# Reordering the first two rows' sums, one transfer's issuer and the first norm in a one-core state-space and MLP kernel

## The chip, the core and the metric

The kernel runs on one core of one Trainium2 chip. The metric is the device time of one execution in microseconds, as the median of several executions; less is better. A profiled execution gives, beside its own time, the span from the first to the last instruction and the record of every instruction.

## What is computed

There are two blocks on a sequence of 2048 positions with 448 channels, cut here to what matters:

```python
x = A_q
h = x + A_ref(layernorm(x), k, v, shift_k, ssm_k, ssm_D)   # q * (long convolution of k_shift*v)
h2 = h + B_ref(layernorm(h), w1, b1, w2, b2)
# B_ref: layernorm, then over the positions: gelu(h^T w1 + b1), 1792 wide, then times w2, plus b2
```

The first block is a causal convolution over all 2048 positions (the reference does it by FFT) of `k_shift * v` with a long filter, plus `kv * ssm_D`, multiplied by the normalised `q`. The second block normalises again, twice in the reference, and runs a two-layer MLP along the positions.

## The kernel before, in words

The 2048 positions lie as 128 partitions by 16 "rows" (R = 16; row r holds the positions 16q + r), each row 448 channels wide. The convolution is done as transforms written as matmuls: stage 1 and stage 2 for the filter and for the input, products, and a first inverse stage ("i1", `emit_products_i1`), which goes over eight pairs of blocks. Each pair's result is copied from PSUM to the SBUF tile TU by ScalarE (line 738) and from there rearranged by SBUF-to-SBUF transfers into the tile TZ (line 1200; for the last pair line 1189). The transfers of one pair but the last carry both halves of the data (h = 0 and 1) in one go; the last pair's go out one for each half and each block of the pair, four in all. Before, GpSimd issues one of these four (h = 1, first block) and SP three (h = 1 second block, then the two of h = 0).

The second inverse stage ("i2", `emit_i2`) makes, for each row r, one sum in PSUM: two matmuls over TZ (line 1299, h = 0 and 1). Rows 0 and 1 (NZ = 2) are special: their share of the last pair isn't moved into TZ, it is added by four more matmuls (line 1307) that read TU in place, with weights EW. "In-place matmuls" means these. Then come, row by row:

- rows 0 to 3: VectorE combines the sum, straight from PSUM, with a normalised x that was prepared ahead (line 1337). What is prepared (XN) is made by ScalarE (line 1269) from statistics (VectorE, lines 1236 and 1238), a power on GpSimd (lines 1244 and 1247), a product on GpSimd (line 1256) and one on VectorE (line 1259).
- rows 4 to 15: ScalarE (for some rows VectorE) first gates the sum from PSUM (line 1316 or 1318), then VectorE combines (line 1326).
- the second norm of the row: for rows 0 and 1 each, VectorE takes statistics (line 1343), aggregates (line 1346) and forms the variance (line 1375), GpSimd takes the power (line 1379), and VectorE writes the normalised row Q (line 1385). The other rows go in pairs: the combine also accumulates a sum, which is read by a short second instruction (DVE_READ_ACCUMULATOR), ScalarE squares with an accumulator (line 1355), GpSimd does the small arithmetic (lines 1365 to 1379), and VectorE writes Q.

From row 8 on, a row's sum may not start before the gate of the row before it has ended (`after=av[-1:]`, line 1301). The MLP's first layer starts while these rows are still made: with each row's Q, TensorE adds that row's share to seven sums in PSUM (line 1432), seven matmuls a row; then the other seven sums (line 1442) and the second layer (line 1453), whose results VectorE adds to x (line 1456) and which go out.

The order of each engine's work is written out by hand in the table `ORDER`: for each engine a list of tokens such as `i2.1:0-1`, that is stage tag, step number and the numbers of the operations in that step. The program issues them on the engine in just this order; waits follow from the data. A small planner runs over these lists with estimated costs only to choose PSUM banks and the order of emission. The tokens that the change touches: in "pe", `ct.1:7` is a transpose of a table, `warm.2` a matmul whose result isn't used, `i2.1` and `i2.2` belong to row 0, `i2.9` and `i2.10` to row 1, `i2.28`, `i2.45`, `i2.17` to rows 4, 7 and 2. In "dve", `q.N` are the statistics of x (`q.7` rows 12 and 13, `q.8` rows 14 and 15; even numbers are the statistics op, odd ones the aggregate), `i2.3` to `i2.8` belong to row 0 (combine 3, statistics 4, aggregate 5, variance 6, norm 8), `i2.11` to `i2.16` to row 1 in the same way, `i2.18` and `i2.21` are the combines of rows 2 and 3, `i2.26` and `i2.27` their norms, `i2.30` and `i2.34` the combines of rows 4 and 5. In "pool" and "sp", `i1.16:19` to `i1.16:22` are the last pair's four transfers, `q.2:5` is the power for rows 2 and 3, `xn.3:0` the product behind it.

Of the kernel before, what the change touches and what calls it, by code (L numbers as in the profile page):

```python
# [39 lines left out]
    ),  # L40
    "act": (
# [24 lines left out]
    ),  # L66
    "pool": (
# [10 lines left out]
    ),  # L78
# [8 lines left out]
    ),  # L87
}

# [493 lines left out]
def _build(nc, A_q, A_k, A_v, A_shift_k, A_ssm_k, A_ssm_D, B_w1, B_b1, B_w2, B_b2, out):  # L583
# [5 lines left out]
    Bsz, S, D = A_q.shape  # L589
# [5 lines left out]
    DB = 2 * D  # L595
# [23 lines left out]
    o_TU = 104064  # L619
# [18 lines left out]
    with ctx:  # L638
        sch = _Sched(nc, ctx, n_dma_sems=112, small_off=SMALL)
        op = sch.op  # L640
# [25 lines left out]
        TU = view(o_TU, [R, 2, D])  # L666
        KN = view(o_KN, [4, S])
        W2 = [view(o, [NFC // 2, S]) for o in o_W2]
        TZ = view(o_TZ, [R, 2, D])
# [3 lines left out]
        ET = view(o_ET, [2 * R, 128], f16)  # L673
# [11 lines left out]
        NZ = 2  # L685
        o_EW = o_I2 + 128
        EW = view(o_EW, [4 * NZ, 128], f16)
# [24 lines left out]
        def Pb(b, i=0):  # L712
            return PS[:, b.slots[i], 0:D]
# [164 lines left out]
        r_ET = lambda r: (o_ET + 512 * r, 512)  # L878
# [271 lines left out]
        def emit_products_i1():  # L1150
            for jj in range(R // 2):
                ms = []
                for h in range(2):
# [10 lines left out]
                       r=[ru, (o_TK + i * 2 * DB, 2 * DB)], bw=[m], n=4 * D, after=aft)  # L1164
# [8 lines left out]
                for h in range(2):  # L1173
                    for t, (tab, xy) in enumerate(((mt[0], 0), (mt[2], 3), (mt[1], 1), (mt[1], 2))):
                        for par in range(2):
                            P = slice(64 * par, 64 * par + 64)
                            k = op("pe", lambda e, W, b=bs[h], m=ms[h], par=par, t=t, tab=tab, xy=xy, P=P: e.matmul(  # L1177
                                Pb(b, par), tab[P, :], MR(m.slots[0])[P, xy, :], start=(t == 0), stop=(t == 3)),
                               r=r_iv if jj < R // 2 - 1 else [(o_ML, 768)], br=[ms[h]], bw=[bs[h]], n=D, est=94.5, mode=3)
# [3 lines left out]
                if jj == R // 2 - 1:  # L1183
                    for h in range(2):
                        for par in range(2):
                            j = 2 * jj + par
                            p0 = 64 * (j & 1) + 32 * ((j >> 1) & 1) + (j >> 2)
                            o_h = o_TU + (2 * j + h) * DB
                            k = op("pool" if h and par == 0 else "sp", lambda e, W, j=j, h=h, p0=p0: e.dma_start(
                                TZ[p0:p0 + 29:4, NZ:R, h, :], TU[0:8 * (R - NZ), j, h, :]),  # L1190
                                   r=[(o_h, DB)], w=[(o_TZ + NZ * 2 * DB, (14 - NZ) * 2 * DB, "zpool"), (o_TZ + 28 * DB, 4 * DB, "zsp")],
                                   dmab=8 * (R - NZ) * DB, keng=8)
                            shuf["zpool"] = k
                            shuf.setdefault("zl", []).append(k)
                    continue
                for par in range(2):
                    j = 2 * jj + par
                    p0 = 64 * (j & 1) + 32 * ((j >> 1) & 1) + (j >> 2)
                    for q_, a, b_, j0 in (("sp" if j in (1, 3, 5, 9, 11) else "pool", 0, 112, 0), ("pool" if jj in (2, 3, 6) else "sp", 112, 128, 14)):
# [3 lines left out]
                           r=[(o_TU + j * 2 * DB, 2 * DB)], w=[(o_TZ + j0 * 2 * DB, (b_ - a) // 8 * 2 * DB, "zsp" if j0 else "zpool")],  # L1203
# [79 lines left out]
        def emit_i2():  # L1283
            sch.t0 = T_M1 + 30.0
            op("pool", lambda e, W: e.tensor_tensor(out=bm, in0=qs[:, :, 0], in1=b2c, op=ALU.add),
               r=[(o_qst, 256), (o_b2c, 64)], w=[(o_bm, 64)], n=16)
            av = []
            first = []
            for g, (r0, ng) in enumerate(GR):
                oh = o_hst + 64 * g  # L1290
                hs = view(oh, [16], f32)
                for i in range(ng):
                    r = r0 + i
                    sch.t0 = T_I2 + T_DI2 * r
                    b = _Buf(psum)
                    A = view(o_TZ + r * 2 * DB, [D], f32)
                    tz = [(o_TZ + r * 2 * DB, 2 * DB)]
                    for h in range(2):
                        k = op("pe", lambda e, W, b=b, r=r, h=h: e.matmul(  # L1299
                            Pb(b), ET[:, 2 * r + h, :], TZ[:, r, h, :], start=(h == 0), stop=(h == 1 and r >= NZ)),  # L1300
                           r=[r_ET(r)] + tz, bw=[b], n=D, after=av[-1:] if r >= 8 and h == 0 else ())
                    if r < NZ:
                        sch.t0 += 0.2
                        for h in range(2):
                            for jx in range(2):
                                j = R - 2 + jx
                                k = op("pe", lambda e, W, b=b, r=r, h=h, j=j, jx=jx: e.matmul(  # L1307
                                    Pb(b), EW[:, 4 * r + 2 * jx + h, :], TU[:, j, h, :], start=False, stop=(h == 1 and jx == 1)),
                                   r=[(o_EW + 1024 * r + 512 * jx + 256 * h, 256), (o_TU + (2 * j + h) * DB, DB)], bw=[b], n=D, safter=(k,))
                    i2_last.append(k)  # L1310

                    sch.t0 += 0.01
# [27 lines left out]
                    if ng == 1:  # L1340
# [3 lines left out]
                           r=hx, w=[(oh + 32, 24)], n=D, kind="1x")  # L1344
# [6 lines left out]
                    else:  # L1351
# [6 lines left out]
                           r=hx, w=[(oh + 8 + 4 * i, 4), (o_JK, DB)], n=D, est=580.0)  # L1358
# [3 lines left out]
                if ng == 2:  # L1362
# [4 lines left out]
                       r=[(oh, 8)], w=[(oh + 16, 8)], est=290.0)  # L1367
                    op("pool", lambda e, W, hs=hs: e.tensor_tensor(out=hs[:, 6:8], in0=hs[:, 4:6], in1=hs[:, 4:6],
                                                                   op=ALU.mult), r=[(oh + 16, 8)], w=[(oh + 24, 8)], est=290.0)
                    op("pool", lambda e, W, hs=hs: e.tensor_tensor(out=hs[:, 8:10], in0=hs[:, 2:4], in1=hs[:, 6:8],  # L1370
                                                                   op=ALU.subtract),
# [10 lines left out]
                for i in range(ng):  # L1382
                    r = r0 + i
# [132 lines left out]
```

## Time and profile before

| | us |
|---|---|
| median of 3 runs | 172.06 |
| lowest and highest of them | 171.93, 172.31 |
| the profiled execution's own time | 172.93 |
| its span, first to last instruction | 171.0 |

Over the span TensorE's matmuls are busy 162.0 us (95%), its weight loads 95.1, VectorE 98.9, ScalarE 92.9 and GpSimd 60.3. The granted TensorE clock is 1.0 throughout. A row of the timeline gives start and duration in us, the engine, the line of the kernel, the operation, what is written and read, and how many like instructions follow one another; a bracket behind it gives idle time of the engine ahead of it and what ended that. PE is TensorE's matmul, PEld its weight load, DVE VectorE, ACT ScalarE, POOL GpSimd, SPq SyncE's queue. Instructions overlap a little in their engine's pipeline, so the step from one start to the next can be shorter than a duration.

### The profile page before, as it was taken

The numbers are of one execution on the slowest core, as the hardware profiler recorded it, in microseconds if no ns is written. First come the engines' busy times: TensorE is split into PE (matmuls) and PEld (weight loads), VectorE is DVE, ScalarE is ACT, GpSimd is POOL, SyncE is SP. The second block draws the span as 40 slices with busy tenths as digits, with TensorE's granted clock in tenths as the row PEclk, the third lists the DMA queues.
The fourth block names the chain that finished last, engine by engine and source line by source line (L and its number), as shares of the span: only waits on it lengthen the run. The fifth ranks groups of instructions, "written<-read, shape, count | busy, mean of one in ns | idle before, by whom it ended". The sixth has DMA issues, their size and how long they took to land.

```text
span 171.0 us, 3568 instructions
## 1 busy us (share of the span) xinstructions
PE 162.0 (95%) x1425; PEld 95.1 (56%) x1425; DVE 98.9 (58%) x187; ACT 92.9 (54%) x133; POOL 60.3 (35%) x154
## 2 busy tenths in 40 slices
PE   6989999988889999999999999999999999999993
PEld 2766745442334443464455555555567777777783
DVE  7988988869699999999968810000003223132232
ACT  3698787998889999999887437321210000000000
POOL 8346627591810496576888820000000000000000
PEclk9999999999999999999999999999999999999999
DMA  5999677675859667665999999970000111101111
GB/s 167 406 310 384 192 246 274 246 281 210 270 147 372 236 182 217 186 185 183 319 361 404 413 419 421 418 324 13 0 0 4 54 54 54 54 0 58 54 54 54
DMA packets 15740, 35.15 MB, mean 206 GB/s; under 512 B 3628, under 2 KB 9980, under 8 KB 15724
## 3 DMA queue, kind: packets, MB, share of 16 engines
q1 hardware_dynamic: 12924, 29.08, 47.2%
q0 software_dynamic: 2656, 5.76, 10.5%
q8 instruction: 11, 0.18, 0.4%
q10 hardware_dynamic: 144, 0.08, 0.2%
q14 instruction: 5, 0.04, 0.1%
HBM read 22.05 MB, written 1.84 MB: 140 GB/s over the span
## 4 chain that ended last, share of the span: by engine, by line
PE 66%; ACT 14%; DMA 12%; DVE 3%; issue 2%; SPq 2%; POOL 0%; DVEq 0%
PE ps L1453 25%; PE ps L1442 12%; PE ps L1432 11%; ACT arena L738 7%; DMA arena<-arena 7%; DMA arena<-in_A_ssm_k_dram 5%; PE ps L1094 5%; ACT arena L1069 4%; PE ps L1177 4%; PE ps L1059 2%; PE ps L1299 2%; ACT arena L1316 2%; PE ps L992 1%; DVE arena L742 1%; PE ps L1307 1%
## 5 line engine op out<-in xcount | busy, mean ns | idle before, releaser
L1456 DVE SCALAR_TENSOR_TENSOR arena<-ps,arena 128x448 bf16<-128x448 f32 (+2 forms) x17 | 11.2, 656 | 57.4 <-PE ps L1453 57.3
L1453 PE MATMUL ps<-arena 128*128 128x448 bf16 (+2 forms) x238 | 42.7, 342 | 0.0
L1453 PEld LDWEIGHTS ps<-arena 128*128 128x128 bf16 x238 | 33.3, 145 | 9.5
L738 ACT CAST arena<-ps 128x896 bf16<-128x896 f32 x30 | 24.6, 1021 | 0.5 <-PE ps L1094 0.5
L1432 PE MATMUL ps<-arena 128*128 128x448 bf16 x112 | 22.5, 353 | 0.0
L1069 ACT CAST arena<-ps 128x896 bf16<-128x896 f32 x24 | 20.5, 915 | 3.7 <-PE ps L1059 3.7
L1075 POOL DMA_DIRECT2D arena<-arena x32 | 17.6, 553 | 12.7 <-ACT arena L1069 11.1
L1442 PE MATMUL ps<-arena 128*128 128x448 bf16 x112 | 21.3, 352 | 0.0
L1422 ACT ACTIVATE arena<-ps,arena 128x448 bf16<-128x448 f32 x14 | 8.2, 639 | 18.7 <-PE ps L1442 14.6
L1094 PE MATMUL ps<-arena 128*64 128x448 bf16 x128 | 15.2, 359 | 2.9 <-ACT arena L1069 0.9
L1160 DVE TENSOR_TENSOR arena<-arena 128x1792 bf16<-128x1792 bf16 x16 | 16.7, 1086 | 0.3 <-ACT arena L738 0.3
L1432 PEld LDWEIGHTS ps<-arena 128*128 128x128 bf16 x112 | 10.8, 98 | 10.6 <-DVE arena L1385 0.9
L1442 PEld LDWEIGHTS ps<-arena 128*128 128x128 bf16 x112 | 11.0, 98 | 10.2
L1059 PE MATMUL ps<-arena 128*32 128x448 bf16 x256 | 15.0, 355 | 0.8 <-DVE arena L1007 0.5
L1177 PE MATMUL ps<-arena 64*128 64x448 bf16 x128 | 14.5, 351 | 0.1
L1200 POOL DMA_DIRECT2D arena<-arena x15 | 8.7, 583 | 13.8 <-ACT arena L738 13.8
L1094 PEld LDWEIGHTS ps<-arena 128*64 128x64 f16 x128 | 6.2, 108 | 10.8 <-ACT arena L738 3.0
L1177 PEld LDWEIGHTS ps<-arena 64*128 64x128 f16 x128 | 6.1, 94 | 8.2 <-ACT arena L738 2.5
L1007 DVE TENSOR_TENSOR arena<-ps,arena 128x512 bf16<-128x512 f32 (+1 forms) x16 | 9.1, 618 | 2.1 <-PE ps L992 1.8
L1355 ACT ACTIVATE arena<-arena 128x448 bf16<-128x448 bf16 x14 | 8.0, 572 | 3.7 <-DVE arena L1326 3.6
L738 ACT COPY arena<-ps 128x1024 bf16<-128x1024 bf16 (+1 forms) x8 | 8.1, 1073 | 3.3 <-PE ps L966 3.3
L1059 PEld LDWEIGHTS ps<-arena 128*32 128x32 f16 x256 | 5.1, 95 | 7.6 <-DVE arena L1007 2.5
(97 smaller groups left out, 194.4 us busy)
## 6 DMA issues: line engine op xcount, KB each, us to landing
arena<-in_B_w_dram SPq DMA_DIRECT2D x8, 896.0 KB, 9.5
arena<-in_B_w_dram SPq DMA_DIRECT2D x2, 2048.0 KB, 17.8
arena<-arena POOLq DMA_DIRECT2D x32, 112.0 KB, 3.1
arena<-arena SPq DMA_DIRECT2D x16, 224.0 KB, 3.3
arena<-in_B_w_dram SPq DMA_DIRECT2D x2, 1536.0 KB, 20.3
arena<-in_A_k_dram SPq DMA_DIRECT2D x4, 448.0 KB, 6.0
arena<-in_A_v_dram SPq DMA_DIRECT2D x4, 448.0 KB, 9.0
arena<-in_A_q_dram SPq DMA_DIRECT2D x4, 448.0 KB, 5.5
```

The lines of the kernel that those rows point to most:

```text
L738: return e.copy(out=dst(), in_=src())
L1007: return e.tensor_tensor(out=v, in0=u.rearrange("p t (r d) -> p t r d", d=64), in1=v, op=ALU.mult)
L1059: op("pe", lambda e, W, b=b, r=r, q=q, x=x, c0=c0: e.matmul(PS[32 * q:32 * q + 32, b.slots[x], 0:D], E[:, 2 * r + x, c0:c0 + 32], src[:, r ...
L1069: return e.copy(out=dst, in_=Ppair(b)) if W == "act" else e.tensor_copy(out=dst, in_=Ppair(b))
L1075: shuf[tag].append(op(q_, lambda e, W, g=g, i=i, a=a, nu=nu, jh=jh: e.dma_start(T[a + i:a + i + 4 * nu - 3:4].rearrange("p (j k) c d -> p ...
L1094: op("pe", lambda e, W, b=bs[h], h=h, j=j, c=c, par=par: e.matmul(PS[64 * par:64 * par + 64, b.slots[c], 0:D], FW[:, 64 * c:64 * c + 64], ...
L1160: op("dve", lambda e, W, m=m, i=i: e.tensor_tensor(out=MR(m.slots[0]).rearrange("p (x y) d -> p x y d", x=2), in0=TU[:, i].unsqueeze(2).br ...
L1177: k = op("pe", lambda e, W, b=bs[h], m=ms[h], par=par, t=t, tab=tab, xy=xy, P=P: e.matmul(Pb(b, par), tab[P, :], MR(m.slots[0])[P, xy, :], ...
L1432: op("pe", lambda e, W, r=r, fc=fc, b=bs[fc]: e.matmul(Pb(b), W1A[:, r, 128 * fc:128 * fc + 128], Q[:, r, :], start=(r == 0), stop=(r == R ...
L1442: op("pe", lambda e, W, r=r, fc=fc, b=b: e.matmul(Pb(b), W1B[:, r, 128 * (fc - n0):128 * (fc - n0) + 128], Q[:, r, :], start=(r == 0), sto ...
L1453: op("pe", lambda e, W, r=r, fc=fc, b=b, d0=d0, d1=d1: e.matmul(Pb(b)[:, d0:d1], W2[fc // 7][:, fc % 7, r:S:R], G[:, fc, d0:d1], start=(fc ...
L1456: op("dve", lambda e, W, r=r, b=b, d0=d0, d1=d1: e.scalar_tensor_tensor(out=X[:, r, d0:d1], in0=Pb(b)[:, d0:d1], scalar=bm[:, r:r + 1], in ...
```

## The change

It has three parts. First, for rows 0 and 1 the four in-place matmuls are issued ahead of the two over TZ, with h = 1 ahead of h = 0, and the first of them opens the sum; TensorE's list has row 0's six, then row 1's six in this order, and the transpose `ct.1:7` goes ahead of them. Second, of the last pair's four transfers GpSimd issues the two of the first block (h = 1, then h = 0), the latter placed ahead of `q.2:5`; SP issues the other two. Third, in VectorE's list the statistics op of row 13 (`q.7:2`) leaves its place ahead of row 0's combine and goes behind the combine of row 5 (`i2.34`); row 0's statistics, aggregate and variance come ahead of row 1's combine; row 0's norm comes ahead of the combine of row 2; and `q.8:2` goes behind the norm of row 2 (`i2.26`).

The diff, cut in the long lists to the tokens that move:

```diff
 "pe":
-ct.2:0-7 warm.12:0 warm.3:0 ct.0:0-7 ct.1:0-6 warm.2:0 i2.1:0-1 i2.2:0-3 i2.9:0 ct.1:7 i2.9:1 i2.10:0-3
+ct.2:0-7 warm.12:0 warm.3:0 ct.0:0-7 ct.1:0-7 warm.2:0 i2.1:0-3 i2.2:0-1 i2.9:0-3 i2.10:0-1
 "dve":
-xn.3:1 q.7:0 q.7:2 i2.3:0 q.6:3 i2.4:0 i2.11:0 i2.5:0
-i2.12:0 i2.6:0 i2.13:0 i2.18:0 i2.14:0 i2.8:0 i2.21:0 i2.16:0 i2.30:0 i2.34:0 q.7:1 q.7:3 q.8:0 q.8:2
-i2.26:0 q.8:1 q.8:3 i2.27:0
+xn.3:1 q.7:0 i2.3:0 q.6:3 i2.4:0 i2.5:0 i2.6:0 i2.11:0
+i2.12:0 i2.13:0 i2.8:0 i2.14:0 i2.18:0 i2.21:0 i2.16:0 i2.30:0 i2.34:0 q.7:2 q.7:1 q.7:3 q.8:0 i2.26:0 q.8:2
+q.8:1 q.8:3 i2.27:0
 "pool":
-q.2:4 i1.16:21 q.2:5
+q.2:4 i1.16:21 i1.16:19 q.2:5
 "sp":
-i1.16:22 i1.16:20 i1.16:19 w1a.1:0
+i1.16:22 i1.16:20 w1a.1:0
@@ emit_products_i1
-k = op("pool" if h and par == 0 else "sp", lambda e, W, j=j, h=h, p0=p0: e.dma_start(
+k = op("pool" if par == 0 else "sp", lambda e, W, j=j, h=h, p0=p0: e.dma_start(
     TZ[p0:p0 + 29:4, NZ:R, h, :], TU[0:8 * (R - NZ), j, h, :]),
@@ emit_i2
-for h in range(2):
-    k = op("pe", lambda e, W, b=b, r=r, h=h: e.matmul(
-        Pb(b), ET[:, 2 * r + h, :], TZ[:, r, h, :], start=(h == 0), stop=(h == 1 and r >= NZ)),
-       r=[r_ET(r)] + tz, bw=[b], n=D, after=av[-1:] if r >= 8 and h == 0 else ())
 if r < NZ:
-    sch.t0 += 0.2
-    for h in range(2):
+    k = None
+    for h in (1, 0):
         for jx in range(2):
             j = R - 2 + jx
             k = op("pe", lambda e, W, b=b, r=r, h=h, j=j, jx=jx: e.matmul(
-                Pb(b), EW[:, 4 * r + 2 * jx + h, :], TU[:, j, h, :], start=False, stop=(h == 1 and jx == 1)),
+                Pb(b), EW[:, 4 * r + 2 * jx + h, :], TU[:, j, h, :], start=(h == 1 and jx == 0), stop=False),
...
+    sch.t0 += 0.2
+for h in range(2):
+    k = op("pe", lambda e, W, b=b, r=r, h=h: e.matmul(
+        Pb(b), ET[:, 2 * r + h, :], TZ[:, r, h, :], start=(h == 0 and r >= NZ), stop=(h == 1)),
+       r=[r_ET(r)] + tz, bw=[b], n=D, after=av[-1:] if r >= 8 and h == 0 else ())
```

More of the change, by code (lines that the diff above doesn't have):

```diff
@@ L1307, in emit_i2 @@
                                 k = op("pe", lambda e, W, b=b, r=r, h=h, j=j, jx=jx: e.matmul(
-                                    Pb(b), EW[:, 4 * r + 2 * jx + h, :], TU[:, j, h, :], start=False, stop=(h == 1 and jx == 1)),
-                                   r=[(o_EW + 1024 * r + 512 * jx + 256 * h, 256), (o_TU + (2 * j + h) * DB, DB)], bw=[b], n=D, safter=(k,))
+                                    Pb(b), EW[:, 4 * r + 2 * jx + h, :], TU[:, j, h, :], start=(h == 1 and jx == 0), stop=False),
+                                   r=[(o_EW + 1024 * r + 512 * jx + 256 * h, 256), (o_TU + (2 * j + h) * DB, DB)], bw=[b], n=D,
+                                   safter=() if k is None else (k,))
+                        sch.t0 += 0.2
[3 more added lines that the diff above has]
+                           r=[r_ET(r)] + tz, bw=[b], n=D, after=av[-1:] if r >= 8 and h == 0 else ())
                     i2_last.append(k)
```

52 rows, old and new, of the table ORDER are left out of this document.

## The prediction, on record before the result was known

> **What bounds the kernel now.** I read the page first (TensorE is busy nearly throughout), then the windows, to find where TensorE stops waiting for anything, then the chain that ended last and the timeline just ahead of that point. The windows count each engine's busy time in a stretch; TensorE is the second column.
>
> ```profile
> core 0 of [0], span 171.0 us
> ...
> 84.12:125.75 41.63, 41.63 (x222) 21.55 (x222) 11.82 (x37) 18.19 (x39) 12.95 (x32) 1.00 0.75 295
> 125.75:168.40 42.65, 42.65 (x239) 33.13 (x237) 10.64 (x16) 0.63 (x1) 0.00 (x0) 1.00 0.11 41
> ```
>
> From 84.12 us on TensorE is full to its last matmul, at a granted clock of 1.00. The work behind that point is the same before and after, so the change is worth just what it moves that point. The timeline ahead of it (start, duration, engine, line, idle time in brackets):
>
> ```profile
> 79.33 0.55 POOL L1379 TENSOR_TENSOR arena<-arena 128x1 f32<-128x1 f32 x1 [0.50 <-DVE arena L1375]
> 79.34 0.65 DVE L1337 SCALAR_TENSOR_TENSOR arena<-ps,arena 128x448 bf16<-128x448 f32 x1
> 79.91 0.08 DVE L1337 DVE_READ_ACCUMULATOR arena<-ps,arena 128x1 f32 x1
> ...
> 79.98 0.39 DVE L1385 TENSOR_SCALAR arena<-arena 128x448 bf16<-128x448 bf16 x1
> 80.03 0.58 ACT L1355 ACTIVATE arena<-arena 128x448 bf16<-128x448 bf16 x1
> ...
> 80.28 0.68 DVE L1337 SCALAR_TENSOR_TENSOR arena<-ps,arena 128x448 bf16<-128x448 f32 x1
> 80.42 0.87 PEld L1432 LDWEIGHTS ps<-arena 128*128 128x128 bf16 x6 [0.45 <-DVE arena L1385]
> ...
> 82.94 0.71 ACT L1316 ACTIVATE arena<-ps,arena 128x448 f32<-128x448 f32 x1
> ...
> 83.70 0.11 PEld L1299 LDWEIGHTS ps<-arena 128*128 128x128 f16 x2 [0.52 <-ACT arena L1316]
> ...
> 83.71 0.55 PE L1299 MATMUL ps<-arena 128*128 128x448 bf16 x2
> ...
> 84.12 1.06 PEld L1432 LDWEIGHTS ps<-arena 128*128 128x128 bf16 x7 [0.30 <-DVE arena L1385]
> ```
>
> Read it backwards. Row 10's sum (83.71) waits for ScalarE's gate of row 9, which ends at 82.94 + 0.71 = 83.65. ScalarE runs without a gap from row 2's square (80.03) to that gate. The square squares what VectorE's combine of row 2 (79.34) writes; the read of that combine's accumulator ends at 79.91 + 0.08 = 79.99, and the square starts 0.04 later. So the chain is: combine of row 2, square, ScalarE's queue, row 10's sum, end. The 0.45 us at 80.42, where TensorE waits for the first norm, lies ahead of the stop at 83.70 and costs nothing of its own.
>
> **The change, part by part.** First the start of the stage: transfers, TensorE and GpSimd.
>
> ```profile
> 72.12 1.87 ACT L738 CAST arena<-ps 128x896 bf16<-128x896 f32 x2
> ...
> 73.20 2.19 SPq L1189 DMA_DIRECT2D arena<-arena  x3
> ...
> 73.47 0.63 POOL L1189 DMA_DIRECT2D arena<-arena  x1 [0.63 <-ACT arena L738]
> ...
> 74.13 0.74 POOL L1247 TENSOR_TENSOR arena<-arena 128x2 f32<-128x2 f32 x1
> ...
> 74.56 0.35 PE L1210 MATMUL ps<-arena 128*128 128x448 f16 x1
> 74.95 0.19 POOL L1256 TENSOR_TENSOR arena<-arena 128x2 f32<-128x2 f32 x1
> ...
> 75.28 0.54 PE L1299 MATMUL ps<-arena 128*128 128x448 bf16 x2 [0.36 <-DMA arena<-arena]
> ...
> 75.42 1.07 POOL L1247 TENSOR_TENSOR arena<-arena 128x4 f32<-128x4 f32 x1
> ...
> 75.65 0.92 PE L1307 MATMUL ps<-arena 128*128 128x448 bf16 x4
> ...
> 77.50 0.95 PEld L1299 LDWEIGHTS ps<-arena 128*128 128x128 f16 x6 [0.18 <-DMA arena<-arena]
> ```
>
> ```profile
> DMA to landing us min/median/max: 2.8/2.8/2.8
> ```
>
> *Matmul order.* Four in-place matmuls start 0.19 us apart (0.92 for four, the last 0.35 long: 0.57 over three starts). They read only what ScalarE's casts leave, so they no longer wait for the landing that holds row 0 until 75.28. The trace has no such start; it is bounded by the last warm-up matmul: 0.25 after its start if a transpose and one slot lie between (74.81), or after its end if the sum gets its PSUM bank (74.56 + 0.35 + some 0.1 = 75.03). I take 75.03, since the old sum too started only behind it. Row 0's last matmul then ends at 75.03 + 5 x 0.19 + 0.35 = 76.33 (early end 76.11), instead of 75.65 + 0.92 = 76.57.
>
> *GpSimd's second transfer.* The casts end at 72.12 + 1.87 = 73.99. SP's three issues take 2.19 (about 0.7 each), so its third starts near 74.72 and lands 2.8 later, at 77.5, which is what TensorE's load of row 4 waits for at 77.50. GpSimd started its issue 0.27 after SP for the same cast. So its second starts at 74.29, takes 0.63, and lands at 77.1: rows 2 and up are 0.4 sooner. But everything queued behind it on GpSimd is later. The power of rows 2 and 3 (L1247) moves from 74.13 to 74.95, the product (L1256) from 74.95 to 75.77; both have readers on VectorE and ScalarE.
>
> ```profile
> 73.70 2.12 ACT L738 COPY arena<-ps 128x1024 f16<-128x1024 f16 x2
> ...
> 75.46 0.13 DVE L1259 SCALAR_TENSOR_TENSOR arena<-arena 128x2 f32<-128x2 f32 x1
> ...
> 75.50 1.14 DVE L1236 BATCH_NORM_STATS2 arena<-arena 128x6 f32<-128x448 bf16 x2
> 75.62 1.46 ACT L1269 ACTIVATE arena<-arena 128x448 f32<-128x448 bf16 x2
> ...
> 76.61 0.68 DVE L1337 SCALAR_TENSOR_TENSOR arena<-ps,arena 128x448 bf16<-128x448 f32 x1
> ...
> 76.94 1.05 ACT L738 COPY arena<-ps 128x1024 f16<-128x1024 f16 x1
> 77.21 0.17 DVE L1238 BATCH_NORM_AGGREGATE arena<-arena 128x2 f32<-128x6 f32 x1
> 77.33 0.63 DVE L1343 BATCH_NORM_STATS2 arena<-arena 128x6 f32<-128x448 bf16 x1
> 77.47 0.24 POOL L1244 TENSOR_SCALAR arena<-arena 128x4 f32<-128x4 f32 x1 [0.97 <-DVE arena L1238]
> ...
> 77.79 1.04 POOL L1247 TENSOR_TENSOR arena<-arena 128x4 f32<-128x4 f32 x1
> 77.87 0.67 DVE L1337 SCALAR_TENSOR_TENSOR arena<-ps,arena 128x448 bf16<-128x448 f32 x1
> ...
> 78.18 0.72 ACT L1316 ACTIVATE arena<-ps,arena 128x448 f32<-128x448 f32 x1 [0.19 <-PE ps L1299]
> ```
>
> *What that wait holds.* L1259 needs the power, which now ends at 75.69: it starts at 75.73 instead of 75.46. Behind it in VectorE's queue stands one statistics op (0.54 start to start) before row 0's combine, where two stood: the combine can start at 75.77 + 0.54 = 76.31. TensorE allows 76.33 + 0.04. I take 76.35, 0.26 sooner than 76.61. ScalarE's two activations (L1269) need the product, so they move from 75.62 to 76.00 and the copy behind them to 77.31; a copy takes about 0.9 start to start (2.12 for two), so the gate of row 4 starts at 78.22 instead of 78.18, although its sum is there sooner. The transfer's gain ends here.
>
> *VectorE's order* is the large term. From row 0's combine to row 2's it now does everything of row 0 first, in a chain where each op needs the one before. An op that needs its predecessor starts 0.04 after that one's end (76.61 + 0.68 = 77.29, then 77.33); one that doesn't starts 0.09 ahead of it (77.33 + 0.63 = 77.96, but 77.87). The sum: combine 0.68 + 0.04; statistics 0.63 + 0.04; aggregate 0.17 + 0.04; variance 0.07 (79.91 to 79.98 holds one such op); combine of row 1 0.67 + 0.04; statistics 0.63 + 0.04; aggregate 0.10; norm of row 0 0.30 (79.98 to 80.28); variance of row 1 0.07: 3.52 us, where before it was 79.34 - 76.61 = 2.73. So row 2's combine starts at 76.35 + 3.52 = 79.87 instead of 79.34: **0.53 us later**.
>
> The norm inside that sum must not wait for its power. GpSimd's group that ends at 75.42 + 1.07 = 76.49 is 0.82 later, 77.31; the next group, 77.79 + 1.04 - 77.47 = 1.36 long if it starts at once, ends near 78.7; the power of row 0 (L1379, 0.55) at about 79.3. VectorE comes to the norm at 79.5. That cover is some 0.15 us; any more delay on GpSimd passes straight to the end.
>
> *The small moves.* The transpose that goes ahead of row 0 is counted above (one slot at 74.75). The statistics op taken from in front of combine 0 comes back behind the combine of row 5, where another one leaves for a place behind the norm of row 2: that norm has as many ops ahead of it as before, and the norm of row 3 one more (0.54), which TensorE needs only after the seven matmuls of the 84.12 row, 1.3 us later. GpSimd's group for rows 4 to 7 ends at 77.31, ahead of the gate of row 4. SP drops an issue and starts its next weight load up to 0.4 sooner; nothing in the stretch waits for it. If one of these covers fell, its price would be its own delay, at most 0.5.
>
> *Sum.* Square of row 2 at 80.56; ScalarE's unbroken queue keeps its length of 83.65 - 80.03; row 10's sum at 84.24. TensorE's work ahead of it starts sooner, but only waits longer there. The second stop, 84.12 for the norm of row 2, hangs on the square of row 3 in the same queue and moves by at most as much. So +0.53: the profiled execution of 172.93 us (span 171.0 and 1.93 around it) would be 173.46. The median of the runs shown, 172.06, lies 0.87 below that execution, so the forecast is 172.06 + 0.53 = 172.59. Its own range, with combine 0 between 76.1 and 76.6, is 172.3 to 172.8.
>
> **One rule weighed.** The rows above price the dependence of one VectorE op on the last at 0.13 us. The Trainium skill, "VectorE: DVE Perf Modes", section "The DRAIN you can't avoid", says that the next op waits for an empty pipe in any case and that a semaphore after each op costs nothing extra. By that rule the chain costs only its ops; the 77.87 row, which starts ahead of its predecessor's end, speaks against it here.
>
> **The rivals.**
>
> *B, the order costs only its ops.* If dependent ops follow like the others, the sum is 2.73 plus the norm (0.30) and a variance (0.07) that now come first: 3.10, combine 2 at 79.45, +0.1: 172.2. The starts above speak against it, the short distance for it.
>
> *C, faster: ScalarE's queue starts sooner.* If combine 2 doesn't end last, the queue starts with row 4's sum. That is ready when its transfer lands: 77.1 against 77.5, so up to 0.4 sooner, 171.65. It decides from the point where combine 2 starts ahead of 79.34 and L1269 isn't late; combine 0 would have to start by 75.84, and row 0's matmuls end only after 76.1. Against it also is that GpSimd's issue delays L1269.
>
> *D, GpSimd's second issue is held or lands late.*
>
> ```profile
> 81.19 0.68 DVE L1326 SCALAR_TENSOR_TENSOR arena<-arena 128x448 bf16<-128x448 bf16 x1
> ...
> 81.45 0.47 POOL L1368 TENSOR_TENSOR arena<-arena 128x2 f32<-128x2 f32 x1
> ...
> 84.02 0.19 POOL L1368 TENSOR_TENSOR arena<-arena 128x2 f32<-128x2 f32 x1
> ```
>
> The same small GpSimd op takes 0.19 alone and 0.47 beside VectorE's combine, ending 0.05 after it. If a statistics op of 0.61 held the issue so, the power, combine 0 and all behind would be up to 0.6 later again: 173.1. The first issue, 0.63 at 73.47 beside such an op, shows no hold. The Trainium skill, "SBUF — State Buffer", section "Who interferes with whom", has GpSimd blocked only by VectorE ops with two SBUF inputs or in a two-port mode, which would clear the statistics ops. A late landing alone is covered: row 4's sum may be 0.4 later before ScalarE, which waits for combine 2, notices.
>
> That the transfer moves without effect (nothing is gained at 77.5) is part of the forecast already.
>
> **Chances.** Forecast 0.62, B 0.16, C 0.11, D 0.11. A measurement of this kernel tells about 0.2%, 0.34 us, from no change. Faster by more: C, 0.11. Within: B and the forecast's low edge, 0.21. Slower: the rest and D, 0.68. The range takes in B, the forecast and the nearer part of D, and the spread of the runs: 171.95 to 172.95.
>
> **What would show it.** Right: combine 2 (the third L1337) near 79.87; ScalarE idle before its first square (L1355), released by VectorE; row 10's sum (L1299) near 84.2; L1259 and L1269 later by 0.3 to 0.4. Wrong: combine 2 at or before 79.4, or a first square that starts right behind the gates. If TensorE showed a new stop behind 84.2, or none at row 10, the whole chain would be misread.

## The result, and the profile after

The changed kernel takes 173.00 us (median of 22 runs, 172.18 to 175.25) where the kernel before takes 172.38 us in the same comparison (22 runs, 171.61 to 173.66). The ratio is 1.0031 with a 95% interval of 1.0016 to 1.0046, that is 0.53 us slower (0.28 to 0.79). The ratio leaves out the run of 175.25 us, whose granted clock was 0.99, so it differs a little from that of the two medians. The prediction was 0.53 us slower. The kernel before measured 0.32 us higher here than in the three runs that were shown, so the absolute 173.00 lies 0.41 above the predicted 172.59 and 0.05 above the upper end of the range, 172.95; with the same 0.32 added, the range is 172.27 to 173.27, and 173.00 lies in it. The difference is what was predicted. The profiled execution of the changed kernel took 173.51 us, span 171.5.

In the changed kernel the lines behind 1290 lie up to two further down: 1303 are the in-place matmuls, 1309 the two over TZ, 1318 the gate, 1328 and 1339 the combines, 1345, 1348, 1377 and 1381 the statistics, aggregate, variance and power of rows 0 and 1, 1357 the square, 1387 the norm, 1434 the MLP's first layer. First the windows of the kernel after, behind the last place where TensorE stops for long:

```profile
84.50:126.18 41.68, 41.68 (x221) 21.48 (x220) 12.09 (x38) 18.12 (x40) 12.12 (x31) 1.00 0.74 291
126.18:168.80 42.62, 42.62 (x239) 33.12 (x237) 10.61 (x16) 0.63 (x1) 0.00 (x0) 1.00 0.11 41
```

TensorE is full from there on as before, with the same work to do (before, two stretches of 41.63 and 42.65 us). So the loss arose ahead of 84.50. The timeline of the kernel after, from the last transfers on:

```profile
72.08 1.87 ACT L738 CAST arena<-ps 128x896 bf16<-128x896 f32 x2
...
74.25 0.60 POOL L1189 DMA_DIRECT2D arena<-arena  x1 [0.19 <-issue]
...
74.77 0.92 PE L1303 MATMUL ps<-arena 128*128 128x448 bf16 x4
74.86 0.74 POOL L1247 TENSOR_TENSOR arena<-arena 128x2 f32<-128x2 f32 x1
...
75.52 0.54 PE L1309 MATMUL ps<-arena 128*128 128x448 bf16 x2
75.63 0.16 DVE L1259 SCALAR_TENSOR_TENSOR arena<-arena 128x2 f32<-128x2 f32 x1
...
75.91 1.41 ACT L1269 ACTIVATE arena<-arena 128x448 f32<-128x448 bf16 x2
...
76.25 0.67 DVE L1339 SCALAR_TENSOR_TENSOR arena<-ps,arena 128x448 bf16<-128x448 f32 x1
...
76.95 0.63 DVE L1345 BATCH_NORM_STATS2 arena<-arena 128x6 f32<-128x448 bf16 x1
...
77.61 0.18 DVE L1348 BATCH_NORM_AGGREGATE arena<-arena 128x2 f32<-128x6 f32 x1
...
77.66 1.10 PE L1309 MATMUL ps<-arena 128*128 128x448 bf16 x5 [0.46 <-DMA arena<-arena]
77.83 0.15 DVE L1377 TENSOR_SCALAR arena<-arena 128x1 f32<-128x1 f32 x1
77.90 0.68 DVE L1339 SCALAR_TENSOR_TENSOR arena<-ps,arena 128x448 bf16<-128x448 f32 x1
```

The time from issue to landing of the two transfers that GpSimd issues:

```profile
DMA to landing us min/median/max: 2.9/3.0/3.1
```

And from where TensorE has row 4's sum to the point from which it is full:

```profile
78.61 0.63 DVE L1345 BATCH_NORM_STATS2 arena<-arena 128x6 f32<-128x448 bf16 x1
...
79.28 0.18 DVE L1348 BATCH_NORM_AGGREGATE arena<-arena 128x2 f32<-128x6 f32 x1
79.38 0.36 DVE L1387 TENSOR_SCALAR arena<-arena 128x448 bf16<-128x448 bf16 x1
79.66 0.15 DVE L1377 TENSOR_SCALAR arena<-arena 128x1 f32<-128x1 f32 x1
79.72 0.67 DVE L1339 SCALAR_TENSOR_TENSOR arena<-ps,arena 128x448 bf16<-128x448 f32 x1
...
80.30 1.30 PE L1434 MATMUL ps<-arena 128*128 128x448 bf16 x6
...
80.44 0.58 ACT L1357 ACTIVATE arena<-arena 128x448 bf16<-128x448 bf16 x1 [0.25 <-DVE arena L1339]
...
81.77 0.55 PE L1309 MATMUL ps<-arena 128*128 128x448 bf16 x2 [0.17 <-ACT arena L1318]
...
83.35 0.71 ACT L1318 ACTIVATE arena<-ps,arena 128x448 f32<-128x448 f32 x1
...
84.11 0.11 PEld L1309 LDWEIGHTS ps<-arena 128*128 128x128 f16 x2 [0.68 <-ACT arena L1318]
```

Read it forwards. What the new orders on TensorE and VectorE were to bring sooner is sooner: row 0's combine starts at 76.25 (before 76.61), its norm at 79.38 (before 79.98), and TensorE takes up the first layer at 80.30 without a stop (before 80.42, behind a stop of 0.45). But the combine of row 2 starts at 79.72 instead of 79.34. ScalarE, which before came to its first square just as the combine ended, now idles for it (0.25 us, released by L1339), and from the square on its queue runs without a gap to the gate of row 9. TensorE's weight load for row 10's sum waits for that gate, 0.68 us instead of 0.52, and the sum starts at 84.12. Row 9's sum (81.77) now has a stop of its own, 0.17 us behind the gate of row 8 in the same queue. It adds nothing, because TensorE stops again for the gate of row 9.

The two executions differ a little ahead of this stage, so distances are taken from the end of ScalarE's last cast of the products: 72.12 + 1.87 = 73.99 before and 72.08 + 1.87 = 73.95 after. Row 10's sum starts 9.72 us behind it before and 10.17 after: **0.45 us later**, which is the loss. The same distance tells the experiments apart below, more finely than their times do: one comparison's interval is 0.4 us to either side.

### The profile page after: what moved, and what is told of

The parts are those of the page before. It is cut to its first block, busy times and chain, and to the rows that moved or that the text cites. A ratio compares the mean times of both kernels' runs of the same rounds, so it can differ in the third digit from the quotient of the medians.

```text
span 171.5 us, 3568 instructions
## 1 busy us (share of the span) xinstructions
PE 162.3 (95%) x1425; PEld 95.1 (55%) x1425; DVE 99.2 (58%) x187; ACT 93.0 (54%) x133; POOL 59.7 (35%) x155
## 4 chain that ended last, share of the span: by engine, by line
PE 64%; ACT 13%; DMA 9%; DVE 6%; POOL 2%; issue 2%; SPq 2%; DVEq 0%; POOLq 0%
PE ps L1455 25%; PE ps L1444 12%; PE ps L1434 11%; ACT arena L738 7%; DMA arena<-in_A_ssm_k_dram 5%; PE ps L1094 5%; DMA arena<-arena 5%; ACT arena L1069 4%; PE ps L1177 4%; PE ps L1059 2%; PE ps L992 1%; PE ps L1309 1%; DVE arena L742 1%; ACT arena L1357 1%; DVE arena L1339 1%
## 5 line engine op out<-in xcount | busy, mean ns | idle before, releaser
L1236 DVE BATCH_NORM_STATS2 arena<-arena 128x6 f32<-128x448 bf16 x16 | 9.4, 610 | 0.0
```

## Experiments

Each kernel was compared with the kernel before in five rounds. The theory is that of the prediction: a chain of dependent VectorE ops makes row 2's combine late, and ScalarE's queue carries that to row 10's sum. Rival 1 puts the loss on the second GpSimd transfer (the prediction's D goes that way), rival 2 counts VectorE's ops but not their dependence (the prediction's B).

### The three parts alone

VectorE's order alone:

```diff
 "dve":
-xn.3:1 q.7:0 q.7:2 i2.3:0 q.6:3 i2.4:0 i2.11:0 i2.5:0 i2.12:0 i2.6:0 i2.13:0 i2.18:0 i2.14:0 i2.8:0 i2.21:0
+xn.3:1 q.7:0 i2.3:0 q.6:3 i2.4:0 i2.5:0 i2.6:0 i2.11:0 i2.12:0 i2.13:0 i2.8:0 i2.14:0 i2.18:0 i2.21:0
```

(and, as in the change, `q.7:2` and `q.8:2` in their later places)

> VectorE's new order alone, with TensorE's and GpSimd's parts as before. Theory (the chain of dependent VectorE ops sets the end): row 0's sum is no sooner than before, so its combine starts at 76.61 again, the combine of row 2 comes 3.5 us behind it, near 80.1 instead of 79.34, ScalarE idles about 0.7 us before its first square, and the kernel is 0.6 to 0.8 us slower than before, more than with all three parts together. Rival 1 (the second GpSimd transfer sets the end): no change, within 0.1 us. Rival 2 (VectorE's order costs only the ops that move, 0.37 us): 0.3 to 0.4 us slower.

Its timeline (the lines are those of the kernel before, less one):

```profile
71.29 1.86 ACT L737 CAST arena<-ps 128x896 bf16<-128x896 f32 x2
...
75.80 0.68 DVE L1336 SCALAR_TENSOR_TENSOR arena<-ps,arena 128x448 bf16<-128x448 f32 x1 [0.52 <-PE ps L1306]
...
79.28 0.67 DVE L1336 SCALAR_TENSOR_TENSOR arena<-ps,arena 128x448 bf16<-128x448 f32 x1
...
79.99 0.58 ACT L1354 ACTIVATE arena<-arena 128x448 bf16<-128x448 bf16 x1 [0.48 <-DVE arena L1336]
...
83.67 0.11 PEld L1298 LDWEIGHTS ps<-arena 128*128 128x128 f16 x2 [0.68 <-ACT arena L1315]
```

VectorE waits 0.52 us for TensorE's six matmuls, then runs the chain: 79.28 - 75.80 = 3.48 us to the combine of row 2. ScalarE idles 0.48, and row 10's sum starts 83.67 - 73.15 = 10.52 behind the cast, 0.80 later than before: more than with all three parts. The time agrees in sign, ratio 1.0031 (1.0008 to 1.0053), 0.54 us, below the range expected, which the interval reaches. No transfer was touched here, so rival 1 falls.

TensorE's order alone (the code of `emit_i2` and the "pe" list as in the change, the rest as before):

> The four in-place matmuls first, alone. Theory: row 0's combine waits for VectorE's own two statistics ops until about 76.58 (before 76.61), so nothing behind it moves, and the time is that of before within 0.1 us, although row 0's sum is ready 0.5 us sooner. Rival 1 says the same. Against both: if TensorE's order were what set the end, 0.4 to 0.5 us faster.

Ratio 0.9989 (0.9971 to 1.0007). Its timeline:

```profile
71.81 1.86 ACT L737 CAST arena<-ps 128x896 bf16<-128x896 f32 x2
...
76.25 0.67 DVE L1338 SCALAR_TENSOR_TENSOR arena<-ps,arena 128x448 bf16<-128x448 f32 x1
...
83.34 0.11 PEld L1308 LDWEIGHTS ps<-arena 128*128 128x128 f16 x2 [0.54 <-ACT arena L1317]
```

Row 0's combine starts 2.58 behind the cast (before 76.61 - 73.99 = 2.62) and row 10's sum 9.67 (before 9.72). As expected, the sooner sum only waits for VectorE.

GpSimd's second transfer alone, and then with TensorE's order:

```diff
-k = op("pool" if h and par == 0 else "sp", lambda e, W, j=j, h=h, p0=p0: e.dma_start(
+k = op("pool" if par == 0 else "sp", lambda e, W, j=j, h=h, p0=p0: e.dma_start(
 "pool":
-i1.16:21 q.2:5
+i1.16:21 i1.16:19 q.2:5
 "sp":
-i1.16:22 i1.16:20 i1.16:19 w1a.1:0
+i1.16:22 i1.16:20 w1a.1:0
```

> GpSimd issues two of the four transfers, alone. Theory: the op at line 1259 waits until about 75.65 instead of 75.46, two statistics ops follow, row 0's combine starts near 76.78 and everything behind it is 0.17 us later: 0.1 to 0.2 us slower than before. Rival 1: all of the loss is here, 0.4 to 0.6 us slower.

> All of the change but VectorE's order. Theory: as with GpSimd's part alone, the combine of row 0 near 76.78 and of row 2 near 79.5, 0.1 to 0.2 us slower than before, so that undoing VectorE's order gives back 0.3 us or more of the loss. Rival 1: 0.4 to 0.6 us slower, as with the whole change.

Ratios 1.0011 (0.9989 to 1.0033) and 1.0021 (0.9997 to 1.0044), neither clear of no change by itself. The timeline of GpSimd's part alone:

```profile
71.65 1.87 ACT L737 CAST arena<-ps 128x896 bf16<-128x896 f32 x2
...
75.20 0.16 DVE L1258 SCALAR_TENSOR_TENSOR arena<-arena 128x2 f32<-128x2 f32 x1
...
76.34 0.67 DVE L1336 SCALAR_TENSOR_TENSOR arena<-ps,arena 128x448 bf16<-128x448 f32 x1
...
83.43 0.11 PEld L1298 LDWEIGHTS ps<-arena 128*128 128x128 f16 x2 [0.52 <-ACT arena L1315]
```

The op that needs the delayed power starts 1.68 behind the cast (before 75.46 - 73.99 = 1.47), row 0's combine 2.82 (before 2.62), row 10's sum 9.91: 0.2 later throughout. With TensorE's order it is the same:

```profile
71.98 1.86 ACT L737 CAST arena<-ps 128x896 bf16<-128x896 f32 x2
...
77.67 2.81 PE L1308 MATMUL ps<-arena 128*128 128x448 bf16 x14 [0.57 <-DMA arena<-arena]
...
83.77 0.11 PEld L1308 LDWEIGHTS ps<-arena 128*128 128x128 f16 x2 [0.53 <-ACT arena L1317]
```

Row 10's sum is 9.93 behind the cast. GpSimd's part costs 0.2 us through its queue, not the 0.4 to 0.6 that rival 1 needs.

### Two more variants

The change without GpSimd's part:

> The change without GpSimd's part. Theory: row 0's combine starts 2.1 us after ScalarE's last cast of the products (before 2.62), set by TensorE's sum and one statistics op; the combine of row 2 comes 3.47 us behind it, at 5.57 (before 5.35), ScalarE's first square near 6.27, and the kernel is 0.2 to 0.25 us slower than before, half of the whole change's loss. Rival 1 (the second GpSimd transfer sets the end): as before.

Ratio 1.0030 (1.0007 to 1.0053); row 10's sum at 10.03 behind the cast (84.28 - 74.25), 0.31 later than before. So leaving out GpSimd's part gives back 0.14 of the 0.45 us, somewhat less than the half expected. ScalarE idles for the square here too:

```profile
72.39 1.86 ACT L737 CAST arena<-ps 128x896 bf16<-128x896 f32 x2
...
77.74 2.82 PE L1308 MATMUL ps<-arena 128*128 128x448 bf16 x14 [0.24 <-DMA arena<-arena]
...
80.61 0.58 ACT L1356 ACTIVATE arena<-arena 128x448 bf16<-128x448 bf16 x1 [0.32 <-DVE arena L1338]
...
84.28 0.11 PEld L1308 LDWEIGHTS ps<-arena 128*128 128x128 f16 x2 [0.68 <-ACT arena L1317]
```

The whole change, with row 0's norm behind the combine of row 2 (against the changed kernel):

```diff
-i2.12:0 i2.13:0 i2.8:0 i2.14:0 i2.18:0 i2.21:0
+i2.12:0 i2.13:0 i2.14:0 i2.18:0 i2.8:0 i2.21:0
```

> The whole change, but row 0's norm goes behind the combine of row 2. Theory: the combine of row 2 comes about 3.2 us behind that of row 0 instead of 3.47; the 0.45 us that dependent ops wait stay, the 0.28 of the norm goes. The first square starts near 6.25 after the last cast (whole change 6.49, before 6.04), and the kernel is 0.2 us slower than before instead of 0.45. If dependence cost nothing (the rival that counts only ops): 2.8 us from combine to combine, and no slower than before.

```profile
70.96 1.86 ACT L737 CAST arena<-ps 128x896 bf16<-128x896 f32 x2
...
75.13 0.67 DVE L1338 SCALAR_TENSOR_TENSOR arena<-ps,arena 128x448 bf16<-128x448 f32 x1
...
78.44 0.68 DVE L1338 SCALAR_TENSOR_TENSOR arena<-ps,arena 128x448 bf16<-128x448 f32 x1
...
79.17 0.58 ACT L1356 ACTIVATE arena<-arena 128x448 bf16<-128x448 bf16 x1 [0.23 <-DVE arena L1338]
...
82.85 0.11 PEld L1308 LDWEIGHTS ps<-arena 128*128 128x128 f16 x2 [0.58 <-ACT arena L1317]
```

From combine to combine it is 3.31 us, not the 3.2 expected and far from rival 2's 2.8: without the norm between them, the variance of row 1 waits for its aggregate, so the norm's place was worth 0.16, not 0.28. Row 10's sum is 10.03 behind the cast, the ratio 1.0027 (1.0004 to 1.0050). Rival 2 falls: the norm isn't there and most of the loss is, 0.31 of 0.45 us. From combine to combine this kernel's VectorE does what it did before and one variance op more (0.07 from start to start), yet takes 3.31 us instead of 2.73; so some 0.5 us is the price of the dependence (an estimate: 3.31 - 2.73 - 0.07).

### The gain without the chain, and what bounds it then

TensorE's order and the moved statistics op, but rows 0 and 1 interleaved on VectorE as before, and SP's three transfers (VectorE's list against the changed kernel's):

```diff
-i2.3:0 q.6:3 i2.4:0 i2.5:0 i2.6:0 i2.11:0 i2.12:0 i2.13:0 i2.8:0 i2.14:0 i2.18:0 i2.21:0
+i2.3:0 q.6:3 i2.4:0 i2.11:0 i2.5:0 i2.12:0 i2.6:0 i2.13:0 i2.18:0 i2.14:0 i2.8:0 i2.21:0
```

> TensorE's new order, SP's three transfers, the statistics op of row 13 moved away as in the change, but rows 0 and 1 interleaved on VectorE as before. Theory: combine of row 0 at 2.1 after the last cast, of row 2 at 4.8 (before 5.35): it no longer holds ScalarE's first square. Then ScalarE's queue is set by row 4's sum, which waits for the transfers as before, so row 10's sum comes at 9.7 as before and the time is that of before within 0.1 us. If instead VectorE alone set the end, 0.5 us faster.

Ratio 0.9998 (0.9976 to 1.0020), and row 10's sum 9.69 behind the cast (83.50 - 73.81):

```profile
71.94 1.87 ACT L737 CAST arena<-ps 128x896 bf16<-128x896 f32 x2
...
77.85 2.08 ACT L1317 ACTIVATE arena<-ps,arena 128x448 f32<-128x448 f32 x3
...
78.83 0.68 DVE L1338 SCALAR_TENSOR_TENSOR arena<-ps,arena 128x448 bf16<-128x448 f32 x1
...
83.50 0.11 PEld L1308 LDWEIGHTS ps<-arena 128*128 128x128 f16 x2 [0.61 <-ACT arena L1317]
```

The combine of row 2 comes at 5.02 behind the cast instead of 5.35 (4.8 was expected), and nothing is gained: VectorE no longer holds ScalarE's queue, but the three gates ahead of the square, those of rows 4, 7 and 5, end 6.12 behind the cast (77.85 + 2.08 - 73.81) where they ended 6.14 behind it before (78.18 + 1.95 - 73.99). So the prediction's rival C, a queue that starts sooner, doesn't come about by the new places on TensorE and VectorE, and the moved transfer doesn't bring row 4's sum forward either (3.71 us behind the cast in the changed kernel, 3.61 before). The queue itself was shortened next:

```diff
 "act":
-i2.42:0 i2.31:0 i2.59:0 i2.35:0
+i2.42:0 i2.59:0 i2.31:0 i2.35:0
```

> As the one before, and on ScalarE the square of row 4 goes behind the gate of row 9. Theory (ScalarE's queue between the gate of row 4 and that of row 9 sets row 10's sum): the gate of row 9 ends 0.56 us sooner, row 10's sum comes 0.3 to 0.45 us sooner, at 9.25 to 9.4 after the last cast, and the kernel is 0.2 to 0.45 us faster than before unless the norm of row 2 or the gate of row 12 becomes a new stop, which would take back up to all of it. If ScalarE's queue isn't the bound: no change.

Its timeline at the sums of rows 10 and 14, with the norm of row 2:

```profile
82.68 0.54 PE L1308 MATMUL ps<-arena 128*128 128x448 bf16 x2
83.16 1.06 PEld L1433 LDWEIGHTS ps<-arena 128*128 128x128 bf16 x7 [0.38 <-DVE arena L1386]
...
89.78 0.13 PEld L1308 LDWEIGHTS ps<-arena 128*128 128x128 f16 x2 [0.45 <-ACT arena L1356]
...
89.81 0.54 PE L1308 MATMUL ps<-arena 128*128 128x448 bf16 x2
```

Row 10's sum has lost its wait, as the theory has it: it starts 9.36 behind the cast, which ends at 73.32 here. But there are two new stops. The norm of row 2 costs 0.10 us at 83.16. Row 14's sum starts at 89.81, where seven steps of 0.19 from 88.28 would give 89.61: 0.20 us, ended by ScalarE's square behind the gate of row 13. (The next expectation calls it row 13's sum. That one, at 87.90, follows the matmuls ahead of it in step, and only its weight load idles.) The time is that of before, 0.9994 (0.9973 to 1.0015). Two further moves against the second stop, and the same with TensorE's old order:

```diff
 "act":
-i2.44:0 i2.48:0 i2.81:0
+i2.44:0 i2.81:0 i2.48:0
 "pool":
-i2.37:0 i2.38:0 q.8:4-5
+i2.37:0 q.8:4 i2.38:0 q.8:5
```

> As the kernel with the square of row 4 behind the gate of row 9, and the square of row 7 goes behind the gate of row 12, with GpSimd's first op for rows 12 to 15 ahead of the power of rows 4 and 5, against the new stop seen there at row 13's sum (0.20 us at 16.5 after the last cast). Theory: that stop shrinks or goes, the 0.10 us wait for the norm of row 2 stays, and TensorE's last matmul starts 0.2 to 0.35 us sooner than before, the kernel is 0.2 to 0.35 us faster. If the stop comes from elsewhere: no better than 0.1 us.

> The same, but with TensorE's part as before (the two matmuls over the rearranged tile first). Theory: row 0's combine starts at 2.62 after the last cast again, the first norm is 0.3 to 0.5 us later than in the other kernel of this pair, and TensorE, which comes to row 10's sum 0.1 to 0.25 us later, gives back that much: 0 to 0.2 us faster than before. If the four in-place matmuls' place is without effect even here: as the other kernel.

Ratios 0.9965 (0.9934 to 0.9995) and 0.9970 (0.9944 to 0.9996): both are faster than the kernel before by 0.5 to 0.6 us, more than expected, with intervals that reach from 0.1 to 1.1, and so faster than the changed kernel, which is clear of the kernel before on the other side. They were not run against the changed kernel itself. In the first of the two the stop at row 14's sum shrank:

```profile
89.44 0.11 PEld L1308 LDWEIGHTS ps<-arena 128*128 128x128 f16 x2 [0.32 <-ACT arena L1317]
...
89.92 0.49 PEld L1433 LDWEIGHTS ps<-arena 128*128 128x128 bf16 x4 [0.36 <-DVE arena L1386]
```

That sum comes 0.03 us late instead of 0.20 (89.44, where 88.08 + 7 x 0.19 = 89.41), but a norm then holds TensorE for 0.09 us (89.92, where 89.44 + 2 x 0.19 = 89.82). From the cast to the end of the span the profile shows 96.9 us (170.0 - 73.12) where it was 97.0 before (171.0 - 73.99). So some 0.1 us of the gain is seen in this stage, less than expected; the times' interval reaches down to that, and what makes up the rest of the 0.5 to 0.6 isn't shown. Between the two kernels no difference shows, so even here the place of the in-place matmuls isn't shown to matter.

## Why the prediction was right, step by step

- **The end is fixed by row 10's sum.** Right. It moved by 0.45 us from the cast, and the ratio stands for 0.53 (0.28 to 0.79). That the time agrees to the hundredth is luck: the combine of row 2 came 5.77 us behind the cast (79.72 - 73.95) where 5.88 was worked out (79.87 - 73.99), and the profile shows 0.45 of the 0.53.
- **The queue that carries the delay.** Right. ScalarE idles for the square of row 2 only where VectorE's new order is in; the idle time of 0.25, 0.48, 0.32 and 0.23 us goes with delays at row 10 of 0.45, 0.80, 0.31 and 0.31. But before the change the combine of row 2 didn't hold that queue alone: the gates ahead of the square ended at about the same time (78.18 + 1.95 = 80.13, the read of the combine's accumulator at 79.99). With the combine 0.33 us sooner (5.02 instead of 5.35) row 10's sum came only 0.03 sooner. So here a delay of that combine passed on to the end, and an advance didn't.
- **VectorE's chain.** Right in mechanism and nearly in size: 3.47 us (76.25 to 79.72) against 3.52 worked out. The rows after show the cost of each dependent start: the statistics op ends at 76.95 + 0.63 = 77.58 and its aggregate starts at 77.61; the second one at 78.61 + 0.63 = 79.24, its aggregate at 79.28. Here the dependent starts lie 0.03 to 0.04 behind the end, while the independent combine at 77.90 starts 0.08 ahead of its predecessor's end at 77.98. The section that the prediction cites from the Trainium skill ("VectorE: DVE Perf Modes", "The DRAIN you can't avoid") says of eight copies that a semaphore after each costs nothing extra. These starts don't bear out the rule that the prediction drew from it, that such a chain costs only its ops. The same section of the Trainium skill also says that a next op that isn't held starts earlier, which the prediction left out. The combine at 77.90 agrees with that.
- **Row 0's combine.** Mis-sized by 0.06: it starts 2.30 behind the cast (76.25 - 73.95) against 76.35 - 73.99 = 2.36. The in-place matmuls started right behind the warm-up (74.77), the early one of the two bounds, so TensorE wasn't in the way, and the wait at line 1259 was shorter (75.63, not 75.73).
- **GpSimd's queue.** Right: the power starts at 74.86 and line 1269 at 75.91 (worked out: 74.95 and 76.00). It is worth 0.2 us alone and 0.14 within the change. The second issue itself took 0.60 us beside VectorE's statistics, so it wasn't held as in rival D.
- **The second transfer's landing.** Wrong: "lands at 77.1: rows 2 and up are 0.4 sooner". GpSimd's two land at most 3.1 us behind their issue, so by 77.35 (74.25 + 3.1). TensorE still waits for a landing, so one of SP's, until 77.66, 3.71 behind the cast, where it was 77.60 - 73.99 = 3.61 before. It cost nothing, because the prediction had ScalarE's copy and then the square in the way of that gain, and they are.
- **The margin at row 0's norm** held: VectorE came to it (79.38) behind its aggregate, not behind the power, which was done at 79.06.

What the runs leave open is why the timed differences of the parts (0.54 us for VectorE's order alone, 0.53 for the whole) don't show the 0.35 us between them that the profiles show; each interval is wider than that. Ahead of the stage, where no edit changes an engine's order, the profiles shown here differ by more than all of these: the cast ends between 72.82 and 74.25 us.

## What to carry to other kernels

Before you bring one row's result forward, look at who waits for the next row on the same engine: finishing row 0 first made VectorE run a chain of dependent ops with nothing to put between them, and the row that another engine's queue was waiting for came later. Two rows interleaved cost less than one after the other (2.73 and 2.87 us from combine to combine, against 3.31 to 3.49). And an early result is worth nothing where it joins a queue that something else holds as well: here no new order on TensorE or VectorE gained anything, and only kernels in which ScalarE's queue itself was shortened measured faster.

## What the runs showed of the hardware that was not expected

Moving one of four transfers of 98 KB from SP's queue to GpSimd's brought its issue forward from 74.73 to 74.25, but not the landing of the four. By the semaphore updates in the traces, what came late was a transfer that wasn't touched, SP's second: with two issues on each engine it landed 3.59 us behind its issue in the changed kernel, and 3.44 to 3.71 in the other three kernels with that part; with three on SP and one on GpSimd it took 2.86 in the kernel before, and 2.77 to 2.89 in the others. What holds it isn't shown. TensorE's next sum shows the same from the other end. With TensorE's new order it starts 3.71, 3.83 and 3.56 us behind the cast with two issues on each engine (the changed kernel, TensorE's and GpSimd's parts together, and the kernel with row 0's norm behind). With three on SP it starts 3.49 behind it (the change without GpSimd's part, 77.74 - 74.25), and 3.56 with TensorE's order alone (77.23 - 73.67): no later, though its last transfer was issued about 0.4 us later.
